# Moving a transpose stage into the arm of a branch, and hinting a jump over empty iterations

## The chip, the cores and the metric

The kernel runs on one core of a Trainium2 chip. The metric is device microseconds of one execution. A core has five engines with an instruction stream each: TensorE (PE, matmuls and transposes, with the loading of weights shown apart as PEld), VectorE (DVE), ScalarE (ACT), GpSimd (POOL) and SyncE (SP, here mostly an issuer of DMAs). A runtime branch is executed by every engine whose code it holds.

## The reference, cut to what matters

Three layers follow each other, in fp32:

```
x = attention(q, k, v)                # blocks of 64 rows
for each batch, for each position s:  # the experts, the stage of this change
    fresh = argmax(logits[s])
    e = fresh if s == 0 or gate[s] < 0.5 else e_of_the_position_before
    out[s] = softmax(logits[s])[e] * (relu(x[s] @ w1[e]) @ w2[e])
out = causal_mix(out)                 # four causal attention experts, top 2
```

There are 8 batches of 576 positions, a model width of 512, 8 experts and an inner width of 1024. Which row goes to which expert is known only at run time.

## The kernel before

The kernel first computes the attention and the routing, then the experts, then the causal mix. The change is in the experts stage, function `experts`.

The rows are sorted by expert into slots of 128 rows, and two slots make a pair. A pair belongs to one expert. The loop `pairs(2, 23)` goes over pairs t = 2 to 22; a second loop over pairs 23 to 27 stands under `tc.If(GO[NP])` (lines 1128 to 1130) for inputs that spread worse; with these inputs it is jumped over. Each pair has a kind, a number computed by the kernel itself and loaded into a register of each engine (`kind`): 0 is two full tiles of 128 rows, 1 the same with a second tile of at most 64 rows, 2 one tile, 3 ("short" below) one tile of at most 64 rows. In the run shown the short pairs are 4, 9, 11, 15 and 19; pairs 14 and 22 are of kind 1 and the others of kind 0. Products are made of two parts: every fp32 operand is split into a high and a low fp32r half (`split`, `relu_split`: one ACT and one DVE operation each), and hi x hi, lo x hi and hi x lo are summed.

The loop body is software-pipelined. In iteration t these steps are issued, in this order on every engine:

- `gather(t+2)` (POOL, indirect DMA), the gate values of t, the kind of t+1 and whether t+1 has a new expert;
- `swap(t-1, 1)`: if pair t-1 has a new expert, its W2 is split on ACT and DVE, and the next one is loaded by SP;
- `up(t)`: the product with W1, `If(KIND[t] < 2)` at line 988. The full arm has 96 matmuls per two tiles (lines 1608 to 1610 of a helper) and splits the result with a relu. The other arm has `one` (line 970), with W1 as the moving operand: 16 matmuls for a short pair, and a copy of each half of the result to `hs` (ACT, line 971). There the result lies with rows on partitions, and must be transposed;
- `x_in(t+1)`: eight transposes of the next pair's x on PE (line 939), and their split (lines 862, 863); `x_fold(t+1)` at line 951;
- `swap(t+1, 0)`: the same as above for W1 of pair t+1;
- `down(t-1)`: tile 0 of the product with W2 (lines 1016, 1018, in the arms of `either`, line 1034), its scaling and an indirect DMA to y (line 1026); then `middle`, which is `h_t` of pair t; then, under `If(KIND[t-1] < 2)` at line 1048, tile 1.

`h_t` stands under a branch of its own, line 975:

```
with tc.If(KIND[t] > 1):
    for js, p in parts:
        for j in range(4):
            nc.tensor.transpose(p[:, j, :], hs[:, ...], self.ident)   # line 978
    with tc.If(KIND[t] > 2) as half:
        ... two copies (ACT, line 981), two adds (DVE, 982), relu and split (955, 956)
```

The tile framework inserts the semaphores between engines. Each engine runs its instructions in order, so what is issued later on an engine waits behind what is issued earlier. In an arm that is not taken the semaphore increments that its instructions would have made are made up for by instructions of its own.

Behind the experts comes `causal_mix`: some masks (POOL, DVE), 30 matmuls on zeros (`keep_warm`, line 158, called at line 1216), and then a list of work in an order that a planner has set; its first loads from y (SP, line 1259) and transposes of them (PE, line 1267) follow.

Of the kernel before, what the change touches and what calls it, by code (L numbers as in the profile page):

```python
# [13 lines left out]
AF = mybir.ActivationFunctionType  # L14
OP = mybir.AluOpType
# [5 lines left out]
def as_f32(ap):  # L21
    return ap.bitcast(F32)
# [91 lines left out]
class Model:  # L114
# [785 lines left out]
    def experts(self, mix):  # L900
        nc, tc = self.nc, self.tc
# [5 lines left out]
        with ExitStack() as ctx:  # L907
# [7 lines left out]
            KIND, NEXT = {}, {}  # L915
            scat = self.scat
            rest = wk.tile([64, DM], F32, name="rest")

            def gather(t):
                XG[t] = [io.tile([128, DM], F32, name="xg", bufs=2 * AHEAD + 2) for _ in range(2)]  # L920
# [33 lines left out]
            def relu_split(hi, lo, src):  # L954
                nc.scalar.activation(hi, src, AF.Relu)  # L955
                nc.vector.scalar_tensor_tensor(lo, src, 0.0, as_f32(hi), op0=OP.max, op1=OP.subtract)  # L956

            def up(t):
                xh, xl = XH[t]
                hh, hl = HH[t] = [wk.tile([128, JF, 256], F32R, name=n, bufs=2) for n in ("hh", "hl")]  # L960
                hs = wk.tile([128, F], F32, name="hs")
                both = hs[:, :512].rearrange("p (j r) -> p j r", j=JF)
                ph = [ps.tile([128, 512], F32, name="ph", bufs=4) for _ in range(4)]
                cols = [slice(0, 4), slice(4, 8)]

                def one(terms):
                    for n, (p, fs) in enumerate(zip(ph, cols)):
                        for i, (x, w) in enumerate(terms):
                            for j in range(JD):
                                nc.tensor.matmul(p, x[:, j, :128], w[:, j, fs], start=i == j == 0, stop=i == len(terms) - 1 and j == JD - 1)  # L970
                        nc.scalar.activation(hs[:, n * 512:(n + 1) * 512], p, AF.Copy)

                def h_t():
                    parts = [(slice(4 * f, 4 * f + 4), p.rearrange("p (j r) -> p j r", j=4)) for f, p in enumerate(ph[2:])]
                    with tc.If(KIND[t] > 1):  # L975
                        for js, p in parts:
                            for j in range(4):
                                nc.tensor.transpose(p[:, j, :], hs[:, (js.start + j) * 128:(js.start + j + 1) * 128], self.ident)
                        with tc.If(KIND[t] > 2) as half:
                            for js, p in parts:  # L980
                                nc.scalar.activation(both[:, js], p[:, :, 64:], AF.Copy)
                                nc.vector.tensor_tensor(both[:, js], both[:, js], p[:, :, :64], op=OP.add)
                            relu_split(hh[:, :, :64], hh[:, :, 64:128], both)
                        with half.Else():
                            for js, p in parts:
                                relu_split(hh[:, js, :128], hl[:, js, :128], p)

                with tc.If(KIND[t] < 2) as two:
                    for c, p in enumerate(ph):
                        p = p.rearrange("p (d n) -> p d n", d=2)  # L990
                        for d in range(2):
                            self.mm3(p[:, d], [(W1[0][:, j, 2 * c + d], W1[1][:, j, 2 * c + d], xh[:, j], xl[:, j]) for j in range(JD)])
                        relu_split(hh[:, 2 * c:2 * c + 2], hl[:, 2 * c:2 * c + 2], p)
                    with tc.If(KIND[t] > 0):
                        nc.scalar.activation(hh[:, :, 192:], as_f32(hl[:, :, 128:192]), AF.Copy)
                with two.Else():
                    with tc.If(KIND[t] > 2) as half:
                        one([(xh, W1[0]), (xh, W1[1])])
                    with half.Else():
                        one([(xh, W1[0]), (xl, W1[0]), (xh, W1[1])])  # L1000
                return h_t

            def down_new(t, last):
                py = ("ph", 4) if last else ("py", 2)
                PY[t] = [[p.tile([128, DM], F32, name=n, bufs=k) for _ in range(2)] for p, (n, k) in ((ps, py), (io, ("ys", 3)))]

            def down(t, middle, ms):
                hh, hl = HH[t]
                py, ys = PY[t]
                pgs = PG[t]  # L1010

                def tile(m, half):
                    ms = slice(m * 128, (m + 1) * 128)
                    for j in range(JF):
                        for h in (hh,) if half else (hh, hl):
                            nc.tensor.matmul(py[m], h[:, j, ms], W2[0][:, j], start=h is hh and j == 0, stop=False)  # L1016
                    for j in range(JF):
                        nc.tensor.matmul(py[m], hh[:, j, ms], W2[1][:, j], start=False, stop=j == JF - 1)  # L1018
                    if half:
                        nc.scalar.activation(rest, py[m][64:], AF.Copy)  # L1020
                    nc.vector.tensor_scalar(ys[m], py[m], pgs[m], None, op0=OP.mult)  # L1021
                    if half:
                        nc.vector.scalar_tensor_tensor(ys[m][:64], rest, pgs[m][:64], ys[m][:64], op0=OP.mult, op1=OP.add)

                def put(m):
                    st = nc.gpsimd.indirect_dma_start(  # L1026
                        out=self.y_d, out_offset=bass.IndirectOffsetOnAxis(ap=self.sidx[:, 2 * t + m:2 * t + m + 1], axis=0),
                        in_=ys[m], in_offset=None, bounds_check=self.N - 1, oob_is_err=False)
                    for s in scat:
                        tc.declare_no_dep(st.ins, s.ins, reason="no two slots hold the same row")  # L1030
                    scat.append(st)

                def either(m, least):
                    with tc.If(KIND[t] < least) as full:
                        tile(m, False)
                    with full.Else():
                        tile(m, True)
                    put(m)

                if t not in KIND:  # L1040
                    for m in ms:
                        tile(m, False)
                        put(m)
                    middle()
                    return
                either(0, 3)
                middle()
                with tc.If(KIND[t] < 2):  # L1048
                    either(1, 1)

# [12 lines left out]
            def swap(t, w):  # L1063
                with tc.If(GO[t]):
                    for f in self.split_pieces((W1, W2)[w], raw[w]):
                        f()
                    load(w, t)

            def pairs(t0, t1):
# [15 lines left out]
                swap(t0, 0)  # L1085
                if first:
                    down_new(t0 - 1, False)
                    down(t0 - 1, lambda: None, [0])
                if not first:
                    swap(t0, 1)  # L1090
                for t in range(t0, t1 + 1):
                    if t + AHEAD < t1:
                        gather(t + AHEAD)
                    if t < t1:
                        gather_p(t)
                    if t + 1 < t1:
                        kind(t + 1)
                        go(t + 1)
                        x_new(t + 1)
                    if t > t0:  # L1100
                        down_new(t - 1, t == t1)

                    middle = lambda: None
                    if t < t1:
                        if extra and t >= t0 + AHEAD:
                            extra.pop(0)()
                        if t > t0 + (not first):
                            swap(t - 1, 1)
                        middle = up(t)
                    if t + 1 < t1:  # L1110
                        x_in(t + 1)
                        x_fold(t + 1)
                        swap(t + 1, 0)
                    if t > t0 or first:
                        down(t - 1, middle, [1] if t == T0 else range(2))
                    else:
                        middle()
                    if t == t1:
                        break
                    if t == T0:  # L1120
                        raw[1] = self.exp_pool.tile([128, JF, DM], F32, name="raw2")
                        load(1, 0)
                    if t == t1 - 1:
                        swap(t, 1)
                    if t == T0 + AHEAD:
                        GO[NP] = flag(self.chg[0:1, NP:NP + 1], [ET.Activation, ET.DVE, ET.Pool, ET.PE, ET.SP])

            pairs(T0, self.NF)
            with tc.If(GO[NP]):
                pairs(self.NF, NP)  # L1130

    def mix_weights(self, pool, tmp):
# [547 lines left out]
```

## Time and profile before

| | |
|---|---|
| median of three runs | 1107.15 us (1105.62 to 1107.49) |
| profiled execution | 1108.88 us |
| its span | 1107.1 us, mean granted clock 0.994 |
| PE busy | 1042.8 us, 94% |
| DVE busy | 684.6 us, 62% |
| ACT busy | 617.6 us, 56% |
| POOL busy | 337.4 us, 30% |

A share of busy time is over the whole span, and several stages with different limits lie in it. An engine that waits is shown with the instruction that released it; "PEq" or "ACTq" as a releaser is that engine's sequencer, which executes branches and semaphore instructions and counts as not busy. The experts stage of pairs 2 to 22 runs from about 240 to 694 us. The granted clock is TensorE's, as a share of full speed.

### The profile page before, as it was taken

The numbers are of one execution on the slowest core, as the hardware profiler recorded it, in microseconds if no ns is written. First come the engines' busy times: TensorE is split into PE (matmuls) and PEld (weight loads), VectorE is DVE, ScalarE is ACT, GpSimd is POOL, SyncE is SP. The second block draws the span as 40 slices with busy tenths as digits, with TensorE's granted clock in tenths as the row PEclk, the third lists the DMA queues.
The fourth block names the chain that finished last, engine by engine and source line by source line (L and its number), as shares of the span: only waits on it lengthen the run. The fifth ranks groups of instructions, "written<-read, shape, count | busy, mean of one in ns | idle before, by whom it ended". The sixth has DMA issues, their size and how long they took to land. (4 is left out here: it accounts for less than half of the span.)

```text
span 1107.1 us, 24188 instructions
## 1 busy us (share of the span) xinstructions
PE 1042.8 (94%) x7947; PEld 922.4 (83%) x7947; DVE 684.6 (62%) x1791; ACT 617.6 (56%) x1533; POOL 337.4 (30%) x586
## 2 busy tenths in 40 slices
PE   7999988999999998999999998999999999999996
PEld 5777766889888877988888887788999999999985
DVE  6678778473443244543633331387888897898884
ACT  7999997312432233423523220276777777777774
POOL 3102244233223223223332221133334333333431
PEclk9999999999999998999999999999999999999999
DMA  9988984124544134434531320345152533425231
GB/s 224 227 236 216 238 244 133 50 85 163 192 157 155 39 118 122 167 108 136 196 130 50 120 97 32 86 111 124 49 125 67 139 73 115 106 68 133 61 84 49
DMA packets 136486, 139.08 MB, mean 126 GB/s; under 512 B 54724, under 2 KB 108024, under 8 KB 134264
## 3 DMA queue, kind: packets, MB, share of 16 engines
q1 hardware_dynamic: 116584, 99.66, 33.2%
q0 software_dynamic: 12592, 35.18, 9.8%
q10 hardware_dynamic: 7136, 2.11, 0.9%
q8 instruction: 86, 1.41, 0.6%
q14 instruction: 88, 0.72, 0.2%
HBM read 89.70 MB, written 29.64 MB: 108 GB/s over the span
## 5 line engine op out<-in xcount | busy, mean ns | idle before, releaser
L1608 PE MATMUL ph<-xh,w 128*128 128x256 f32 x512 | 142.8, 279 | 6.0 <-ACTq L1048 5.2
L1610 PE MATMUL ph<-xh,w 128*128 128x256 f32 x512 | 142.5, 278 | 0.4 <-issue 0.4
L1609 PE MATMUL ph<-xl,w 128*128 128x256 f32 x512 | 142.4, 278 | 0.0
L955 ACT ACTIVATE hh<-ph 128x512 fp32r<-128x512 f32 x64 | 37.4, 598 | 183.1 <-PE ph L1610 165.3
L1026 POOL DMA_INDIRECT y_d<-ys,sidx x39 | 39.4, 1010 | 298.9 <-DVEq L975 180.4
L1016 PE MATMUL py<-w,hh 128*128 128x512 f32 x280 | 106.0, 403 | 4.7 <-PEq L975 4.7
L1441 POOL TENSOR_SCALAR a<-a,st,g_out 128x128 f32<-128x128 f32 (+3 forms) x128 | 79.0, 617 | 85.4 <-DVE st L1436 58.0
L956 DVE SCALAR_TENSOR_TENSOR hl<-ph,hh 128x512 fp32r<-128x512 f32 x64 | 43.2, 688 | 98.2 <-ACT hh L955 61.4
L1608 PEld LDWEIGHTS ph<-xh,w 128*128 128x128 f32 x512 | 96.2, 188 | 9.0 <-ACTq L1048 6.8
L1021 DVE TENSOR_SCALAR ys<-py,pg 128x512 f32<-128x512 f32 x37 | 27.7, 749 | 112.0 <-PE py L1018 64.6
L1610 PEld LDWEIGHTS ph<-xh,w 128*128 128x128 f32 x512 | 96.8, 189 | 0.1
L1609 PEld LDWEIGHTS ph<-xl,w 128*128 128x128 f32 x512 | 96.1, 188 | 0.5
L1425 ACT ACTIVATE a<-sc,st 128x256 f32<-128x256 f32 (+4 forms) x160 | 82.9, 520 | 19.7 <-DVE st L1417 14.1
L1016 PE MATMUL py<-w,hl 128*128 128x512 f32 x232 | 91.0, 392 | 0.0
L1417 DVE TENSOR_REDUCE st<-sc 128x1 f32<-128x256 f32 (+4 forms) x160 | 75.8, 482 | 4.4
L1240 ACT ACTIVATE at<-tp 128x128 fp32r<-128x128 f32 (+2 forms) x144 | 65.1, 455 | 23.2 <-PE tp L1458 21.2
L1241 DVE TENSOR_TENSOR at<-tp,at 128x128 fp32r<-128x128 f32 (+2 forms) x144 | 72.3, 505 | 7.6 <-ACT at L1240 6.4
L1458 PE MATMUL tp<-ident,a 128*128 128x128 f32 (+1 forms) x400 | 69.9, 277 | 7.0 <-DVE at L1241 3.4
L863 DVE TENSOR_TENSOR w<-raw,w 128x512 fp32r<-128x512 f32 (+1 forms) x84 | 67.1, 866 | 14.5 <-ACT w L862 11.1
L1018 PE MATMUL py<-w,hh 128*128 128x512 f32 x280 | 69.8, 392 | 0.0
L1016 PEld LDWEIGHTS py<-w,hh 128*128 128x128 f32 x280 | 52.4, 189 | 19.0 <-issue 8.9
L1406 PE MATMUL sc<-kd,qs 128*128 128x128 f32 (+3 forms) x256 | 62.7, 337 | 4.9 <-ACT a L1425 3.4
(338 smaller groups left out, 2922.3 us busy)
## 6 DMA issues: line engine op xcount, KB each, us to landing
raw<-in_moe_w_dram SPq DMA_DIRECT2D x32, 1024.0 KB
kd<-kb SPq DMA_DIRECT2D x64, 160.0 KB
vb<-in_v_dram SPq DMA_DIRECT2D x144, 64.0 KB
x_d<-xs POOLq DMA_DIRECT2D x36, 256.0 KB
yt<-y_d SPq DMA_DIRECT2D x32, 256.0 KB
kd<-kb SPq DMA_DIRECT2D x64, 128.0 KB
out_dram<-zs SPq DMA_DIRECT2D x32, 256.0 KB
q<-in_q_dram SPq DMA_DIRECT2D x11, 512.0 KB
```

The costliest lines, as they stand in the source:

```text
L863: (engine or self.nc.vector).tensor_tensor(lo, src, as_f32(hi), op=OP.subtract)
L1016: nc.tensor.matmul(py[m], h[:, j, ms], W2[0][:, j], start=h is hh and j == 0, stop=False)
L1018: nc.tensor.matmul(py[m], hh[:, j, ms], W2[1][:, j], start=False, stop=j == JF - 1)
L1240: h = plan.add("ACT", act(n), lambda: A.activation(hi, src(), AF.Copy), key, dep)
L1241: l = plan.add("DVE", dve(n), lambda: V.tensor_tensor(lo, src(), as_f32(hi), op=OP.subtract), key, [h])
L1417: V.tensor_reduce(st[:, i:i + 1], box["sc"][i][:, :k1 - k0], axis=AX.X, op=OP.max, negate=True)
L1425: A.activation(a[:, k0:k1], box["sc"][i][:, :k1 - k0], AF.Exp, bias=st[:, 0:1], accum_out=st[:, 3 + i:4 + i])
L1441: (P if ext <= PX else V).tensor_scalar(a[:, :ext], a[:, :ext], st[:, 6:7], gate, op0=OP.mult, op1=OP.mult)
L1458: nc.tensor.transpose(ta[:c1 - c0, kc - k0], box["a"][:, c0:c1], self.ident)
L1608: self.nc.tensor.matmul(out, ah, bh, start=first and i == 0, stop=False)
L1609: self.nc.tensor.matmul(out, ah, bl, start=False, stop=False)
L1610: self.nc.tensor.matmul(out, al, bh, start=False, stop=last and i == n - 1)
```

## The change

The transposes of the next pair's x move from behind `up(t)` into both arms of its branch: `up` gets them as a function `then`, called at the end of each arm. `h_t` moves from the middle of `down(t-1)` to the end of the arm for one tile, directly behind them, and loses its own `If`; `down` loses its `middle`. So in a short pair, h_t's transposes, copies, adds and relu are issued before the W1 swap and before the down projection's first tile; in a full pair nothing is left of it. The list of all five engines gets a name, and the branch over pairs 23 to 27 gets a label and a hint: ahead of the last down projection of the first loop a hint instruction on each of the five engines names that branch and the register that decides it. The causal stage is unchanged.

```diff
-            def up(t):
+            def up(t, then):
...
 
                 def h_t():
                     parts = [(slice(4 * f, 4 * f + 4), p.rearrange("p (j r) -> p j r", j=4)) for f, p in enumerate(ph[2:])]
-                    with tc.If(KIND[t] > 1):
+                    for js, p in parts:
+                        for j in range(4):
+                            nc.tensor.transpose(p[:, j, :], hs[:, (js.start + j) * 128:(js.start + j + 1) * 128], self.ident)
+                    with tc.If(KIND[t] > 2) as half:
                         for js, p in parts:
-                            for j in range(4):
-                                nc.tensor.transpose(p[:, j, :], hs[:, (js.start + j) * 128:(js.start + j + 1) * 128], self.ident)
-                        with tc.If(KIND[t] > 2) as half:
-                            for js, p in parts:
-                                nc.scalar.activation(both[:, js], p[:, :, 64:], AF.Copy)
-                                nc.vector.tensor_tensor(both[:, js], both[:, js], p[:, :, :64], op=OP.add)
-                            relu_split(hh[:, :, :64], hh[:, :, 64:128], both)
-                        with half.Else():
-                            for js, p in parts:
-                                relu_split(hh[:, js, :128], hl[:, js, :128], p)
+                            nc.scalar.activation(both[:, js], p[:, :, 64:], AF.Copy)
+                            nc.vector.tensor_tensor(both[:, js], both[:, js], p[:, :, :64], op=OP.add)
+                        relu_split(hh[:, :, :64], hh[:, :, 64:128], both)
+                    with half.Else():
+                        for js, p in parts:
+                            relu_split(hh[:, js, :128], hl[:, js, :128], p)
...
                 with tc.If(KIND[t] < 2) as two:
                     for c, p in enumerate(ph):
@@ -993,18 +993,20 @@
                         relu_split(hh[:, 2 * c:2 * c + 2], hl[:, 2 * c:2 * c + 2], p)
                     with tc.If(KIND[t] > 0):
                         nc.scalar.activation(hh[:, :, 192:], as_f32(hl[:, :, 128:192]), AF.Copy)
+                    then()
                 with two.Else():
                     with tc.If(KIND[t] > 2) as half:
                         one([(xh, W1[0]), (xh, W1[1])])
                     with half.Else():
                         one([(xh, W1[0]), (xl, W1[0]), (xh, W1[1])])
-                return h_t
+                    then()
+                    h_t()
...
-            def down(t, middle, ms):
+            def down(t, ms):
...
-                    middle()
                     return
                 either(0, 3)
-                middle()
                 with tc.If(KIND[t] < 2):
                     either(1, 1)
...
-                    middle = lambda: None
                     if t < t1:
                         if extra and t >= t0 + AHEAD:
                             extra.pop(0)()
                         if t > t0 + (not first):
                             swap(t - 1, 1)
-                        middle = up(t)
+                        up(t, lambda: t + 1 < t1 and x_in(t + 1))
                     if t + 1 < t1:
-                        x_in(t + 1)
                         x_fold(t + 1)
                         swap(t + 1, 0)
+                    if t == t1 and first:
+                        tc.mark_branch_hint_location("more", hint=GO[NP], engines=TAIL)
                     if t > t0 or first:
-                        down(t - 1, middle, [1] if t == T0 else range(2))
-                    else:
-                        middle()
...
             pairs(T0, self.NF)
-            with tc.If(GO[NP]):
+            with tc.If(GO[NP], label="more"):
                 pairs(self.NF, NP)
```

## Rows read from the trace of the kernel before

**Rows 1.** Page, part 1: busy us of each engine (share), instructions.

```profile
PE 1042.8 (94%) x7947; PEld 922.4 (83%) x7947; DVE 684.6 (62%) x1791; ACT 617.6 (56%) x1533; POOL 337.4 (30%) x586
```

**Rows 2.** Waits of PE, 262 to 704 us: total, times, longest.

```profile
PE ph L1608 <- ACTq L1048: 5.2, 4, 1.5
PE tp L158 <- DVEq L1129: 4.8, 1, 4.8
PE py L1016 <- PEq L975: 4.7, 10, 0.6
PE ph L970 <- ACT w L862: 3.7, 1, 3.7
```

**Rows 3.** Line 975, PE's sequencer: count, ns min/median/max, first and last start.

```profile
L975 PEldq EVENT_SEMAPHORE  x16: 51/51/51, 269.0 to 673.6; - x16
```

**Rows 4.** Timeline of PE, pairs 3 and 4: start, us, line, [idle <-releaser].

```profile
288.77 0.49 PE L1016 MATMUL py<-w,hh 128*128 128x512 f32 x1 [0.44 <-PEq L975]
...
304.51 1.04 PE L978 MATMUL ph<-ident,hs 128*128 128x128 f32 x8
305.30 0.48 PE L1016 MATMUL py<-w,hh 128*128 128x512 f32 x1
```

**Rows 5.** Timeline of PE, start of pair 6.

```profile
327.93 0.36 PE L1608 MATMUL ph<-xh,w 128*128 128x256 f32 x1 [1.26 <-ACTq L1048]
```

**Rows 6.** Timeline of PE, start of pair 11, and pair 15.

```profile
430.46 2.00 PE L1018 MATMUL py<-w,hh 128*128 128x512 f32 x8
436.12 6.34 PE L970 MATMUL ph<-w,xh 128*128 128x512 f32 x16 [3.65 <-ACT w L862]
442.30 1.11 PE L939 MATMUL pxt<-ident,xg 128*128 128x128 f32 x8
...
520.02 3.83 PE L970 MATMUL ph<-w,xh 128*128 128x512 f32 x16
```

**Rows 7.** Stretch: length, busy us of PE, PEld, DVE, ACT, POOL, clock, DMA, GB/s.

```profile
436.12:442.30 6.18, 6.18 (x17) 4.81 (x17) 4.99 (x8) 3.99 (x8) 4.01 (x4) 0.56 0.82 250
```

**Rows 8.** Line 988, PE's branch, columns as in rows 3.

```profile
L988 PEldq COMPARE_BRANCH  x21: 65/71/2867, 247.4 to 652.9; - x21
```

**Rows 9.** Timeline of ACT, 434 to 443 us.

```profile
435.24 4.27 ACT L862 ACTIVATE w<-raw 128x512 fp32r<-128x512 f32 x8 [2.08 <-DVEq L1048]
439.87 0.60 ACT L971 ACTIVATE hs<-ph 128x512 f32<-128x512 f32 x1 [0.36 <-ACT w L862]
```

**Rows 10.** Timelines of ACT, DVE and PE, pair 15 and start of 16.

```profile
526.02 3.90 ACT L862 ACTIVATE w<-raw 128x1024 fp32r<-128x1024 f32 x4 [0.50 <-DVE xl L863]
530.84 0.77 ACT L981 ACTIVATE hs<-ph 128x256 f32<-128x256 f32 x2 [0.91 <-PE ph L978]
533.10 0.63 ACT L955 ACTIVATE hh<-hs 128x512 fp32r<-128x512 f32 x1 [1.49 <-DVE hs L982]
...
527.12 4.63 DVE L863 TENSOR_TENSOR w<-raw,w 128x1024 fp32r<-128x1024 f32 x4 [0.82 <-ACT w L862]
...
532.33 0.74 DVE L982 TENSOR_TENSOR hs<-hs,ph 128x256 f32<-128x256 f32 x2
...
534.71 0.28 PE L1608 MATMUL ph<-xh,w 128*128 128x256 f32 x1
```

**Rows 11.** Line 1129, sequencers of PE and DVE, columns as in rows 3.

```profile
L1129 PEldq COMPARE_BRANCH  x1: 3456/3456/3456, 684.9 to 684.9; - x1
...
L1129 DVEq EVENT_SEMAPHORE  x2: 21/21/21, 693.7 to 693.8; - x2
```

**Rows 12.** Timelines of DVE and PE, end of the expert stage.

```profile
690.42 0.74 DVE L1023 SCALAR_TENSOR_TENSOR ys<-rest,pg,ys 64x512 f32<-64x512 f32 x1
...
693.76 8.34 PE L158 MATMUL tp<-zeros 128*128 128x512 bf16 x30 [4.85 <-DVEq L1129]
```

**Rows 13.** Stretches before the causal stage, columns as in rows 7.

```profile
699.00:699.60 0.60, 0.60 (x5) 0.24 (x4) 0.00 (x0) 0.00 (x0) 0.19 (x2) 1.00 0.35 133
699.60:700.20 0.60, 0.60 (x4) 0.26 (x3) 0.00 (x0) 0.00 (x0) 0.00 (x0) 1.00 0.05 17
```

More of the change, by code (lines that the diff above doesn't have):

```diff
@@ L917, in experts @@
             rest = wk.tile([64, DM], F32, name="rest")
+            TAIL = [ET.Activation, ET.DVE, ET.Pool, ET.PE, ET.SP]
             def gather(t):
@@ L1087, in pairs @@
                     down_new(t0 - 1, False)
-                    down(t0 - 1, lambda: None, [0])
+                    down(t0 - 1, [0])
                 if not first:
@@ L1108, in pairs @@
                             swap(t - 1, 1)
-                        middle = up(t)
+                        up(t, lambda: t + 1 < t1 and x_in(t + 1))
                     if t + 1 < t1:
-                        x_in(t + 1)
                         x_fold(t + 1)
                         swap(t + 1, 0)
+                    if t == t1 and first:
+                        tc.mark_branch_hint_location("more", hint=GO[NP], engines=TAIL)
                     if t > t0 or first:
-                        down(t - 1, middle, [1] if t == T0 else range(2))
-                    else:
-                        middle()
+                        down(t - 1, [1] if t == T0 else range(2))
                     if t == t1:
@@ L1125, in pairs @@
                     if t == T0 + AHEAD:
-                        GO[NP] = flag(self.chg[0:1, NP:NP + 1], [ET.Activation, ET.DVE, ET.Pool, ET.PE, ET.SP])
+                        GO[NP] = flag(self.chg[0:1, NP:NP + 1], TAIL)
             pairs(T0, self.NF)
-            with tc.If(GO[NP]):
+            with tc.If(GO[NP], label="more"):
                 pairs(self.NF, NP)
```

## The prediction

> **What bounds the kernel now.** I read the busy shares of the page first: TensorE (PE) is busy 94% of the span and the next engine, VectorE (DVE), 62% [rows 1]. So a microsecond counts only if PE stands idle or slow in it, and the page is not fine enough for that. The list of PE's waits over the expert stage (262 to 704 us) gives what there is to win: 4.7 us in ten waits at line 975, 5.2 us in four waits at line 1048, one wait of 3.7 us before line 970, and one of 4.8 us at the end of the stage, with little beside them [rows 2]. The reader is to see that nearly all of PE's idle time in the stage ends at a branch or at an arm that is jumped over, and little of it at data. The change touches each of these four places.
>
> **Part 1, the skipped arm of line 975 goes away.** Pairs 2 to 22 run here. Five are short (4, 9, 11, 15, 19); in the other sixteen the arm of line 975 is skipped, and the skip is not free: each engine then runs a semaphore instruction in the arm's place, on PE sixteen times [rows 3]. It is put down to PE's own queue: PE waits there until its own earlier matmuls have ended. The ordinary case is the first row of [rows 4]: tile 1 of the down projection starts 0.44 us after the last matmul of tile 0, where matmuls otherwise overlap. Where the arm is taken (pair 4) there is no such gap: the eight transposes of line 978 start at 304.51, last 1.04, and tile 1 starts at 305.30, before they have ended [rows 4]. So the cost is the drain at the skip, 0.47 us on average (4.7 over ten). After the change both arms hold real work (the full arm ends in the transposes of the next x, the short one in h_t's), so no arm without instructions is left at this place. That gives -4.7 us. PE's work as such is the same: the x transposes are issued once in whichever arm runs, h_t's eight likewise. Bounds: 0 if the drain shows up at another join, -4.7 if not; a loss is excluded, as no instruction is added on the path. I take -4.7, since the taken arm's row shows a join without a gap.
>
> In the six skips not among the ten, the next PE work is not tile 1 of the same pair. One (in pair 2) is covered by a wait for weights. In the five others the pair before was short, so the skip of line 975 is followed by that of line 1048: PE drains twice, loads the next pair's kind and branches before it gets work. Four of these end in the waits of line 1048, 5.2 us in all; the first is [rows 5], 1.26 us. The change takes away one of the two drains and leaves the other. The second drain finds PE empty anyway, so what goes is one semaphore instruction and one branch in series. The nearest row prices that at 0.47 as in the ten; the bounds are 0 and the whole 1.26. I take 0.47 x 4 = -1.9 us.
>
> **Part 2, the fifth of these, before pair 11.** Here pair 9's half tile has drained PE and pair 11 is short, so PE must also jump over the whole full arm. Its last matmul ends at 430.46 + 2.00 = 432.46, and the 16 matmuls of line 970 start at 436.12, 3.65 us later; they then take 6.34 us where the same 16 of pair 15 take 3.83 [rows 6]. [...] The wait is put down to a ScalarE copy of line 862 that was long done, so it is something that this row doesn't name. A jump that takes long is the best candidate: the PE branch of line 988 has a median of 71 ns but once took 2867 [rows 8]. The change removes the drain of line 975 ahead (-0.5 us), but the jump over the full arm remains and becomes longer, by the eight transposes now in that arm. I keep the stall: -0.5 us. If it vanishes, PE starts some 2.8 us earlier at full clock, but then h_t can't run at once: it needs the copies of line 971, and ScalarE splits the new W2 from 435.24 for 4.27 us before it makes the first of them at 439.87 [rows 9]. PE would have reached h_t near 438 and would wait until about 440.5 for it. Of the 2.8 + 2.5 us about 2.5 stay. So this place lies between -3 and 0.
>
> [...]
>
> **Part 3, h_t and the W1 swap.** In a short pair h_t now comes before the W1 swap (all five short pairs are followed by a new expert). ScalarE's and VectorE's part of it: two copies of 0.77 us together, two adds of 0.74, the relu of 0.63 [rows 10], a chain of 2.1 us now ahead of the swap instead of behind it. Does PE wait for it? The tightest is pair 15: the swap runs on ScalarE from 526.02 and on VectorE from 527.12 for 4.63, until 531.75; pair 16 starts at 534.71 [rows 10]. Shifted by 2.1 it ends at 533.85, with 0.9 us to spare. So this costs nothing; if the cover were gone, it would be as many tenths as the swap is later than 2.1 + 0.9 us. PE itself must wait for the second copy of line 971 (0.6 us) before the second half of h_t; the eight x transposes (1.1 us) lie between. Cost 0, bounds 0 to +0.5 a pair. On SyncE (SP) and GpSimd (POOL) there is nothing in the moved code but the branch; POOL's scatters are issued behind one branch fewer.
>
> **Part 4, the hint for the jump over pairs 23 to 27.** VectorE's last work ends at 690.42 + 0.74 = 691.16, and its first semaphore instruction behind the jump runs at 693.7; PE stands until 693.76 for that and nothing else, 4.85 us in all [rows 11, 12]. PE's own branch (3456 ns at 684.9) lies beside matmuls that it had already queued. If the hint makes VectorE's target ready, PE's warming matmuls (30, 8.34 us) start at about 691.3, or 2.4 us earlier. What is late next is the first block of y for the causal stage: its loads wait for the last scatter, which the hint doesn't move, and their traffic runs at 133 GB/s until 699.60 and at 17 after it [rows 13]. The warming ends at 702.1 now and would end at 699.7, so both fit: -2.3 us. Bounds: 0 (no effect) to -2.9 (the block that is needed first has landed by 699.0, and the warming is over by then). The row with VectorE's 2.5 us between branch and next instruction is the nearest one, so I take -2.3. [...]
>
> **Sum.** -4.7 - 1.9 - 0.5 - 2.3 = -9.4 us. Against the profiled execution (1108.88, of which 1107.1 is the span) that is 1099.5; the median of the three runs lies 1.7 lower, at 1107.15, and from it I get 1097.7. The causal stage behind is as before and only starts earlier.
>
> **Rivals.**
> [...]
> 2. The stall before pair 11 goes as well. For it: every instruction behind the first pair moves in memory, and such a stall was seen at one of five places only. Against: the jump is longer. Time: 2.5 lower, 1095.2.
> 3. The drains of line 975 come back in another place, as the full arm and the short arm end in different instructions and one of them is evened out by a semaphore instruction behind the x transposes. For it: such instructions stand in every skipped arm. Against: behind the short arm the x transposes follow without a gap today (442.30, before the last of line 970 has ended [rows 6]), though the arms are unequal. [...]
> 4. Slower: the late W1 swap stalls PE at the start of all five pairs behind short ones. For it: relu and adds of h_t cross between ScalarE and VectorE, and the swap stands behind the last of them. The price of one place is the wait and, if PE drops to the low clock as in [rows 7], the 2.5 us that 6.34 against 3.83 shows. It decides from 9.4 / 5 = 1.9 us a place, that is from a swap 2.1 + 0.9 + 1.9 = 4.9 us later than now without a drop of the clock; with 2 us of wait and the drop it is 5 x 4.5 - 9.4 = 13 us slower, 1120. Against: the chain of rows is 2.1 us, and pair 15 alone has as little room as 0.9.
>
> **How the numbers follow.** Forecast 0.52, rival 1 0.18, rival 2 0.12, rival 3 0.10, rival 4 0.05, remainder (mixtures, small losses) 0.03. The range runs from 1094.5 (rival 2 with the larger gain of the hint) to 1103 (rival 1 with a wait of 1 us at three of the pairs of part 3), and leaves out most of rivals 3 and 4. A measurement of this kernel can tell about 0.2%, 2.2 us, from no change: faster (under 1104.9) is the forecast, rivals 1 and 2 and half of rival 3, 0.88; same 0.06; slower 0.06.
>
> **What would show it.** Right: PE's waits for its own queue at line 975 are gone and nothing of 0.4 us stands ten times in their place; the four waits of line 1048 are near 0.8 us each; the warming matmuls start within 0.3 us of VectorE's last work; PE starts pairs 5, 10, 12, 16 and 20 without waiting for a weight copy. Wrong: a drain behind the x transposes (rival 3), VectorE still 2.5 us late behind the last jump (rival 1), waits for line 863 ahead of line 1608 in those five pairs (rival 4), a new long stall before a short pair's line 970. A time over 1104.9 makes the prediction wrong as a whole.

## The result, and the profile after

The changed kernel takes 1090.57 us (1088.82 to 1091.69, five runs) where the kernel before takes 1105.62 in the same series: 0.9859 of it, interval [0.9844, 0.9873], 15 us less. The forecast was 1097.7, the lower end of the range 1094.5. The direction and the places were right and the size was not; 5.6 us were missing, on a forecast of 9.4.

The profiled execution took 1090.41 us. First the engines (busy us, share, instructions), to be read beside [rows 1]:

```profile
PE 1039.2 (95%) x7947; PEld 922.9 (85%) x7947; DVE 684.7 (63%) x1791; ACT 617.1 (57%) x1533; POOL 336.8 (31%) x586
```

PE has the same 7947 matmuls, and yet 3.6 us less busy time: the first hint that more went than the idle time shows. The waits of PE from 262 to 704 us (total, times, longest), beside [rows 2]:

```profile
PE ph L1606 <- ACTq L1048: 3.4, 4, 0.9
PE tp L158 <- DVEq L1127: 2.6, 1, 2.6
PE ph L971 <- ACTq L1048: 1.5, 1, 1.5
PE ph L978 <- ACT hs L972: 1.2, 1, 1.2
```

The reader is to see four things. The ten waits for PE's own queue are gone and nothing has come in their place. The four places behind a short pair have fallen from 5.2 to 3.4 us. The wait before pair 11 is 1.5 and not 3.7 us. And there is one new wait, of 1.2 us, for `hs` (line 978 is h_t's transposes). The matmul lines have moved by two: 1606 to 1608 are the former 1608 to 1610, 1018 and 1020 the former 1016 and 1018.

What the skipped arm had cost is seen best where tile 0 meets tile 1. The timeline of PE in pair 6, first before, then after (start us, length, [idle before it <- released by]):

```profile
344.71 0.85 PE L1018 MATMUL py<-w,hh 128*128 128x512 f32 x3
346.02 0.49 PE L1016 MATMUL py<-w,hh 128*128 128x512 f32 x1 [0.45 <-PEq L975]
346.35 0.40 PE L1016 MATMUL py<-w,hl 128*128 128x512 f32 x1
```

```profile
339.84 1.08 PE L1020 MATMUL py<-w,hh 128*128 128x512 f32 x4
340.76 0.39 PE L1018 MATMUL py<-w,hh 128*128 128x512 f32 x1
340.99 0.39 PE L1018 MATMUL py<-w,hl 128*128 128x512 f32 x1
```

After the change a matmul starts every 0.23 us though one lasts 0.39, as they overlap. Before, the last of the three of line 1018 started at about 345.17 (346.02 - 0.45 - 0.40), and from there to the first of tile 1 it was 0.85 us, and 0.33 to the next. Against 0.23 and 0.23 that is 0.62 + 0.10 = 0.72 us, where the idle column says 0.45. The rest is booked as busy time: the tail of the last matmul and the slow first one overlap with nothing.

Pair 11 after the change, beside [rows 6], and ScalarE there, beside [rows 9]:

```profile
425.70 3.92 PE L971 MATMUL ph<-w,xh 128*128 128x512 f32 x16 [1.45 <-ACTq L1048]
429.46 1.11 PE L940 MATMUL pxt<-ident,xg 128*128 128x128 f32 x8
431.77 1.15 PE L978 MATMUL ph<-ident,hs 128*128 128x128 f32 x8 [1.21 <-ACT hs L972]
433.17 0.47 PE L1018 MATMUL py<-w,hh 128*128 128x512 f32 x1 [0.24 <-issue]
```

```profile
426.82 4.28 ACT L862 ACTIVATE w<-raw 128x512 fp32r<-128x512 f32 x8 [1.88 <-PE ph L971]
431.12 1.08 ACT L972 ACTIVATE hs<-ph 128x512 f32<-128x512 f32 x2
```

There is no stall of 3.7 us and no low clock: the 16 matmuls take 3.92 us, and from 425.70 to 429.46 the granted clock is 1.00. h_t waits for the copies that stand behind the split of W2, as part 2 had it for a stall that goes, but 1.2 us and not 2.5.

The W1 swap of pair 15 on VectorE and the first PE work of pair 16, beside [rows 10]:

```profile
516.42 4.63 DVE L863 TENSOR_TENSOR w<-raw,w 128x1024 fp32r<-128x1024 f32 x4 [1.00 <-ACT w L862]
```

It ends at 521.05 and pair 16 starts at 521.70 without a wait; 0.65 us to spare, 0.9 were forecast. The last jump, beside [rows 11, 12], VectorE's first semaphore instruction behind it and PE's warming matmuls:

```profile
L1127 PEldq COMPARE_BRANCH  x1: 351/351/351, 668.1 to 668.1; - x1
...
L1127 DVEq EVENT_SEMAPHORE  x2: 21/21/21, 674.6 to 674.8; - x2
```

```profile
673.67 0.74 DVE L1025 SCALAR_TENSOR_TENSOR ys<-rest,pg,ys 64x512 f32<-64x512 f32 x1
```

```profile
674.73 8.34 PE L158 MATMUL tp<-zeros 128*128 128x512 bf16 x30 [2.56 <-DVEq L1127]
```

VectorE's last work ends at 674.41 and PE starts 0.3 us later; before it was 2.6 us. With the hint VectorE's first semaphore instruction behind the jump runs at 674.6, 0.2 us after its last work, instead of 2.5, and PE's own branch takes 351 ns instead of 3456, hidden both times behind matmuls that run to 672.16 and 688.92.

### The profile page after: what moved, and what is told of

Same layout as the page of the kernel before. It is cut to its first block, busy times and chain, and to the rows that moved or that the text cites. A ratio compares the mean times of both kernels' runs of the same rounds, so it can differ in the third digit from the quotient of the medians.

```text
span 1088.6 us, 23980 instructions
## 1 busy us (share of the span) xinstructions
PE 1039.2 (95%) x7947; PEld 922.9 (85%) x7947; DVE 684.7 (63%) x1791; ACT 617.1 (57%) x1533; POOL 336.8 (31%) x586
## 5 line engine op out<-in xcount | busy, mean ns | idle before, releaser
L863 DVE TENSOR_TENSOR w<-raw,w 128x512 fp32r<-128x512 f32 (+1 forms) x84 | 67.1, 866 | 15.7 <-ACT w L862 11.2
L862 ACT ACTIVATE w<-raw 128x512 fp32r<-128x512 f32 (+1 forms) x84 | 57.3, 762 | 16.7 <-DMA wst<-in_moe_wq_dram 6.0
```

The lines of the kernel that those rows point to most:

```text
L863: (engine or self.nc.vector).tensor_tensor(lo, src, as_f32(hi), op=OP.subtract)
```

## Experiments

Each ran against the kernel before, in four series, each on a chip of its own by the record: e1 to e4 in series 1, e5 to e8 in series 2, r1, e9, e10 and e12 in series 3, e13, e14 and r2 in series 4. In series 1 and 3 the kernel before takes 1105.9 and 1105.7 us, in series 2 and 4 1111.3 and 1111.8. Times are compared within a series; across series only the ratios to the kernel before are, and with care.

**The hint alone, the move alone** (series 1).

```diff
+ tc.mark_branch_hint_location("more", hint=GO[NP], engines=TAIL)   # e1: added to the kernel before
- tc.mark_branch_hint_location("more", hint=GO[NP], engines=TAIL)   # e2: taken from the changed kernel
```

> The kernel before with the label and the hint alone; x_in, h_t and the branch of line 975 as they were. Theory (the drains at skipped arms are most of the gain, the hint is the small part): VectorE's 2.5 us behind the last jump go, PE's idle time ahead of the warming matmuls falls from 4.8 to about 2.5 us, the ten waits at line 975 stay at 4.7 us and the stall before pair 11 at 3.7; the time is 2.3 to 2.7 us lower, about 1103. Rival A (the hint brings the 5.6 us that the forecast lacked): about 1097. Rival B (the hint does nothing): 1105.6.

> The changed kernel without the hint and the label. Theory: all drains of line 975 gone, the stall before pair 11 gone as in the changed kernel (the hint stands behind that place in the program), VectorE 2.5 us late behind the last jump as before: 2.3 to 2.7 us above the changed kernel, about 1093. Rival A (the hint brings the excess): about 1099. Rival B (the hint does nothing): 1090.6.

e1 takes 1103.24 us, 0.998 [0.9969, 0.9991]; its ten waits at the skipped arm are there (4.9 us), and PE's wait before the warming is 2.5. e2 takes 1093.26, 0.989 [0.9876, 0.9904]. So the hint is worth about 2.6 us and the move 12.6, and they add up to the 15. The move was forecast at 7.1, so the excess over the forecast is in it.

**One half of the move at a time** (series 1). e3 puts x_in into both arms and leaves h_t in the middle under its branch; e4 moves h_t and leaves x_in behind the join.

```diff
-                        middle = up(t)
+                        middle = up(t, lambda: t + 1 < t1 and x_in(t + 1))   # e3; h_t and its If as before
...
-                    then()
-                    h_t()
+                    h_t()          # e4; x_in(t + 1) again behind up(t)
```

> The kernel before with x_in in both arms of the branch of up, and nothing else: h_t stays in the middle of the down projection under its branch at line 975, no hint. Theory (drains): the ten waits at the skipped arm stay at 4.7 us, so no gain from them; only the stall before pair 11 may go, as code moves: 1105.6 or, without the stall, 1101 to 1103. Rival (the transposes of x in the arms are themselves a gain, by a join fewer on the path of the transposes): at least 5 us lower, 1100 or less, with the waits at line 975 in place.

> The changed kernel with x_in back behind the join of the branch of up, so h_t stands in the short arm directly behind the product, no hint. Theory: no skipped arm is left in the middle, so the ten drains are gone (7 us by the distance from matmul to matmul, 0.72 a place), but in the five short pairs PE has no x transposes to do while ScalarE copies the second half of the product (0.6 us and the way there), so it stands about 0.8 us in each, 4 us in all: 1105.6 - 7 - 1.5 + 4 = about 1101, or 1098.5 if the stall before pair 11 goes. Rival (the gain comes with the x transposes in the arms): near 1105.

e3: 1101.37 us, 0.9964 [0.9951, 0.9977]. Waits of PE and the start of pair 11:

```profile
PE py L1018 <- PEq L975: 4.5, 10, 0.5
PE ph L970 <- DVE ys L1023: 1.8, 1, 1.8
```

```profile
430.46 3.92 PE L970 MATMUL ph<-w,xh 128*128 128x512 f32 x16 [1.84 <-DVE ys L1023]
```

The drains are all there, and 4.2 of the 4.5 us come from pair 11 (34.18 us from the start of pair 10 to that of pair 12, 38.41 before): the stall is 1.8 instead of 3.7 us, and the 16 matmuls take 3.92 instead of 6.34. The full stall was gone although the jump over the full arm had become longer. e4: 1098.41 us, 0.9931 [0.9918, 0.9944], near the theory without the stall (1098.5). No drain is left, but five waits for `hs` come up, 3.0 us in all, 0.25 in four pairs and 2.0 in pair 11. The x transposes between product and h_t are PE's cover for ScalarE's copy: e4 differs from e2 in their place alone and is 5.2 us slower.

**The same program, its code elsewhere** (series 2). 64 matmuls on PE in an arm that is never taken, ahead of the loop.

```diff
                     down_new(t0 - 1, False)
+                    with tc.If(KIND[t0] > 1):
+                        self.keep_warm(PY[t0 - 1][0][0], 64)
```

> The kernel before with 64 matmuls on PE in an arm that is never taken, ahead of the loop over pairs: nothing that runs in the loop changes, but its PE code lies 128 or more instructions further on. Theory (the stall before pair 11 hangs on where the code lies): the wait of 3.7 us there falls under 2, the slow clock behind it goes, pairs 10 and 11 together take some 4 us less; the drains stay at 4.7 us; about 1102 with some 0.7 for the skipped arm. Rival (the stall comes from what waits there: the drain of line 975 and ScalarE's order): 3.7 us as before, 1106.

1109.31 us against 1111.29, 0.9981 [0.9969, 0.9993]. Pair 11:

```profile
437.37 5.50 PE L970 MATMUL ph<-w,xh 128*128 128x512 f32 x16 [1.85 <-DVE ys L1021]
```

The stall is halved with nothing else changed ahead of it, so half of it hangs on where the code lies. The expected 4 us didn't come, only 2: the slow stretch is still there in part (5.50 us), and pair 5 now has small issue waits of its own.

**A skipped arm put back, for PE alone** (series 2).

```diff
                 either(0, 3)
+                with tc.If(KIND[T0] > 1):
+                    self.keep_warm(py[1], 1)
                 with tc.If(KIND[t] < 2):
```

> The changed kernel with a branch on PE in the middle of the down projection whose arm (one matmul on zeros) is never taken, in all 21 pairs: only PE gets a skip back, ScalarE and VectorE do not. Theory (a skip costs PE the distance 0.84 to 0.95 instead of 0.23 us from matmul to matmul and a slow second one, 0.72 together): 15 places with a tile 1 behind them by 0.72 and five behind a short pair by 0.36, +12.6 us, about 1103. Rival A (the skip costs what the idle column shows, 0.47 and 0.4): +9, 1099.6. Rival B (most of the gain came from ScalarE and VectorE being free of the skip): +3 or less.

1109.71 us, 0.999 [0.9976, 1.0003]. The changed kernel didn't run in this series; e7 below, which differs from it in the hint's engines alone, takes 1099.11. So some 11 us are lost to a branch that only PE pays for. Its waits:

```profile
PE py L1018 <- PEq L1048: 7.3, 15, 0.7
```

The idle column shows 7.3 us in 15 places, 0.49 each, while the iterations of full pairs are 0.7 to 0.9 us longer than those of the changed kernel (23.75 to 22.89 between the starts of pairs 7 and 8). Rival B is out. The time lies between rival A (9 us) and the theory (12.6) and can't tell them apart; the lengths of the iterations, 0.7 to 0.9 longer where the idle column shows 0.49, speak for the theory.

**The hint on VectorE alone** (series 2).

```diff
- hint=GO[NP], engines=TAIL
+ hint=GO[NP], engines=[ET.DVE]
```

> The changed kernel with the hint on VectorE alone. Theory (PE's start behind the last jump waits for VectorE only, and VectorE's instructions were what was late): as the changed kernel, 1090.6, PE's idle time ahead of the warming matmuls 2.6 us. Rival (the hint on PE or ScalarE matters): 1092 to 1093.3, as without a hint.

1099.11 us, 0.9901 [0.9888, 0.9914]; the changed kernel in series 4, on a chip with a like time of the kernel before, 0.9893 [0.9872, 0.9914]. The sequencers at the last jump:

```profile
L1127 DVEq EVENT_SEMAPHORE  x2: 21/21/21, 681.2 to 681.4; - x2
L1127 ACTq EVENT_SEMAPHORE  x2: 17/17/17, 681.6 to 681.7; - x2
...
L1127 PEldq COMPARE_BRANCH  x1: 3669/3669/3669, 674.7 to 674.7; - x1
L1127 ACTq COMPARE_BRANCH  x1: 50/50/50, 679.0 to 679.0; - x1
L1127 DVEq COMPARE_BRANCH  x1: 85/85/85, 680.6 to 680.6; - x1
```

PE's branch is long again and ScalarE is 2.6 us late again, but VectorE is not, and PE's wait before the warming is 2.6 us as with all five. By the waits VectorE is the one that counts; the times of two series alone would not show it.

**No empty arm behind a short pair, three ways.** e8 (series 2) puts both tiles of the down projection into one branch, e10 (series 3) is e8 with its code moved as in e5, e9 (series 3) gives PE one matmul on zeros in an else arm of line 1048. r1 is the changed kernel beside them, e12 the changed kernel with its code moved (both series 3).

```diff
-                with tc.If(KIND[t] < 2):             # e8, e10
+                with tc.If(KIND[t] < 2) as two:
+                    tile(0, False)
+                    put(0)
                     either(1, 1)
+                with two.Else():
+                    either(0, 3)
...
                 with tc.If(KIND[t] < 2) as two:      # e9
                     either(1, 1)
+                with two.Else():
+                    self.keep_warm(py[1], 1)
```

> The changed kernel with the down projection's two tiles in one branch: tile 0 and tile 1 in the arm for two tiles, the half or single tile in the other, so that the branch of line 1048 has no skipped arm left behind a short pair. Theory: the waits of 3.4 us in four and 1.5 us in one place go, and with them the distance lost from matmul to matmul (about 1.1 us a place and 1.5 for pair 11): 5 to 6 us lower, 1085. Rival A (PE must load the kind and branch there anyway, and stands for it): 1 to 2 us lower, 1089. [...]

> The kernel with both tiles of the down projection in one branch, its PE code 128 instructions further on (64 matmuls in an arm that is never taken, ahead of the loop). [...] Rival (the long arms themselves stall): the wait of 3.4 us behind pair 15 stays, and the time is within 2 us of the changed kernel or above it.

> The changed kernel with one matmul on zeros in an else arm of line 1048, so that PE, and PE alone, skips no empty arm behind a short pair. Theory (an arm with an instruction needs no semaphore instruction that waits for PE's own queue): the waits of 3.4 us in four places and 1.5 in one fall to what ScalarE's skip leaves (it runs some 0.7 us behind PE's last matmul), 2 to 5 us lower than the changed kernel. Rival A (PE stands there for ScalarE's copy of the half tile and not for its own queue): within 1 us of the changed kernel, same waits. Rival B (the matmul's arm costs more than the skip): 1 to 2 us higher.

> The changed kernel with its PE code 128 instructions further on in the same way (about 0.7 us for the skipped arm). Theory (what the forecast lacked at pair 11 hangs on where the code lies, the drains don't): no waits at skipped arms in the middle of the down projection, as in the changed kernel; the start of pair 11 and other starts may stall by 1 to 4 us each; 1 to 6 us above the changed kernel, or the same if no stall comes up. Rival (pair 11's stall went for good with the drain of line 975): 0.7 us above, no stall over 1.5 us at pair 11.

> The changed kernel once more, beside the variants of it. [...] Rival (a good part of the first result is luck of one build on one chip): 10 us or less.

e8: 1102.01 us, 0.9912 [0.9895, 0.9929], 2.9 us above e7 beside it. The waits of line 1048 are gone, but others are new, the longest of them these:

```profile
PE py L1018 <- issue: 3.7, 2, 3.4
...
PE ph L978 <- ACT hs L972: 2.2, 1, 2.2
```

The wait of 3.4 us lies in the down projection of pair 15. In e10 it is gone, and one of 2.9 before pair 15's product has come up instead: 1093.55 us, 0.9896 [0.9877, 0.9914], above r1 with 1089.69, 0.9855 [0.984, 0.9871]. r1 is 16.0 us under the kernel before beside it, so its rival is out. So such a stall moves with the code: e8 is slower than e7, where its theory and rival A had it faster, and in e10 the stall doesn't stay behind pair 15 as the rival had it, though e10's time is no better. e9: 1089.22 us, 0.9852 [0.9835, 0.9869], not to be told from r1. Its waits of line 1048 are gone, and in pair 11 h_t waits for `hs` 2.7 us instead of 1.2, as PE is there sooner and ScalarE is not; the transposes then take 1.97 us instead of 1.15.

The gain behind the short pairs is partly lost again: pair 6 starts 15.60 us behind pair 5 (16.57 in r1), but pair 7 23.47 behind pair 6 (22.97), and from pair 10 to pair 12 it is 36.75 (35.73). The transposes of pair 11:

```profile
431.65 1.97 PE L978 MATMUL ph<-ident,hs 128*128 128x128 f32 x8 [2.66 <-ACT hs L972]
```

e12: 1090.67 us, 0.9861 [0.9838, 0.9883]: the gain of the change doesn't hang on one placing of its code; pair 11 has no stall over 1.5 us in it, as the rival said.

**The drain taken away, h_t left where it was** (series 4). e13 is the kernel before with an else arm at line 975; e14 is the same with e9's else arm and the hint; r2 is the changed kernel.

```diff
-                    with tc.If(KIND[t] > 1):
+                    with tc.If(KIND[t] > 1) as many:
...
+                    with many.Else():
+                        self.keep_warm(ph[0], 1)
```

> The kernel before with an else arm at line 975 that holds one matmul on zeros for PE, and nothing else: h_t stays where it was, ScalarE and VectorE still skip, no hint. Theory (the cost is PE's drain in an arm without an instruction, not the place of h_t): the ten waits for PE's own queue at line 975 go; 0.72 us less and 0.23 more for the matmul in each, so 5 us lower, 1100.5, plus or minus what the stall before pair 11 does. Rival (the arm's semaphores for ScalarE and VectorE hold PE up, or h_t's place is what counts): waits at tile 1 stay, time within 1.5 us of the kernel before.

> The same, with one matmul on zeros in an else arm of line 1048 too, and the hint: the kernel before with all its empty PE arms filled, h_t left in the middle of the down projection. Theory: 5 us from line 975, 4 times about 1.1 and 1.5 from line 1048, 2.6 from the hint, and in pair 11 h_t does not wait for ScalarE's split of W2 as it does in the changed kernel: 13 to 15 us lower than before, 1091, within 2 us of the changed kernel; below it if the stall before pair 11 goes. Rival (moving h_t into the arm is worth something by itself): 3 us or more above the changed kernel.

> The changed kernel beside these two: 1089 to 1091 where the kernel before takes 1105.7.

e13: 1101.07 us, 0.9891 [0.987, 0.9912], 10.7 us less with one matmul more in each pair that isn't short. The waits of line 975 are gone; pair 11 starts after 1.4 us, and its 16 matmuls take 3.92 us. By the profiles (that of before is from another series) the ten places make some 5 us of it (23.19 us from pair 6 to pair 7, 23.70 before), and pair 11, whose stall also moves with the code, 4.4 (33.99 from pair 10 to pair 12, 38.41 before):

```profile
PE ph L1610 <- ACTq L1050: 3.3, 4, 0.8
PE ph L970 <- DVE ys L1023: 1.4, 1, 1.4
```

e14: 1091.8 us, 0.9819 [0.9804, 0.9834], the lowest ratio of all; r2 beside it 1099.16, 0.9893 [0.9872, 0.9914]. The pair 11 of e14:

```profile
432.46 2.19 PE L971 MATMUL ph<-w,xh 128*128 128x512 f32 x8
434.84 2.09 PE L971 MATMUL ph<-w,xh 128*128 128x512 f32 x8 [0.18 <-DVEq L976]
```

PE goes from the half tile into pair 11 without a stop, and h_t, still behind tile 0, finds its copies made. Rival out: with h_t left in the middle the kernel isn't 3 us above the changed one but 7.4 below it. Not all of that is h_t's place, as the changed kernel lacks the else arm of line 1048; with it, it is e9, which ran in another series (0.9852). In pair 11 the moved h_t costs its wait: from pair 10 to pair 12 it is 32.97 us in e14, 36.75 in e9 and 36.17 in r2. r2 missed its expectation, which was written for series with a faster kernel before; in series 4 the change brings 12.7 us. Why less than the 15 to 16 of the other series stays open.

## Why the prediction was right and where it was wrong

**Part 1, the skipped arm: right in mechanism, mis-sized.** The step that failed is "So the cost is the drain at the skip, 0.47 us on average (4.7 over ten)", and with it the bound of 4.7. The idle column gave the size, and it counts from the end of a matmul that would have overlapped with the next. From start to start a drain costs 0.72 us, and the ten together 7.5 (the two tiles take 11.49 to 11.70 us from the first start to the last before, 10.76 to 10.85 after), so 2.8 us were missing. The changed kernel's loop shows it: pair 6 to pair 7 took 23.70 us (327.93 to 351.63) and takes 22.95 (323.31 to 346.26). e6 and e13 show it from both sides. The semaphore instruction in the arm's place runs sixteen times each on PE (51 ns), ScalarE (17) and VectorE (21), not on every engine.

**The skip in pair 2: put at nothing, wrong.** "One (in pair 2) is covered by a wait for weights" failed. From the start of pair 2 to that of pair 3 it took 18.78 us (251.06 to 269.84) and takes 17.77 (248.39 to 266.17). Here is the start of pair 3 on PE and VectorE's split of its W1, first before, then after:

```profile
267.02 1.98 PE L1018 MATMUL py<-w,raw 128*128 128x512 f32 x8
269.84 0.36 PE L1608 MATMUL ph<-xh,w 128*128 128x256 f32 x1 [0.84 <-DVE w L863]
...
266.03 4.63 DVE L863 TENSOR_TENSOR w<-raw,w 128x1024 fp32r<-128x1024 f32 x4 [0.67 <-ACT w L862]
```

```profile
264.35 1.98 PE L1020 MATMUL py<-w,raw 128*128 128x512 f32 x8
266.17 0.28 PE L1606 MATMUL ph<-xh,w 128*128 128x256 f32 x1
...
263.21 4.63 DVE L863 TENSOR_TENSOR w<-raw,w 128x1024 fp32r<-128x1024 f32 x4 [0.68 <-ACT w L862]
```

After the change pair 3 starts 2.96 us behind the start of the split, and without a wait. By that the weights would have let it start at 268.99 before, when PE's matmuls ended (269.00); PE's semaphore instruction of line 975 runs there, at 269.0 [rows 3], and pair 3 starts 0.84 us later. So the wait was put down to the wrong engine, and this skip cost 1.0 us. The four kernels with the empty arm of line 975 show 18.78 to 18.87 us here (before, e1, e3, e5), all others 17.77 to 17.82.

**The four places behind short pairs: right.** Forecast 1.9, measured 1.8 by the waits (5.2 to 3.4). The second drain does remain.

**Part 2, pair 11: wrong.** "I keep the stall: -0.5 us" failed; rival 2 came about. From the start of pair 10 to that of pair 12 it took 38.41 us and takes 35.72, so 2.7 and not 0.5. Under it lies a misread row, "A jump that takes long is the best candidate". The long branch of [rows 8] stands ahead of pair 9, beside queued matmuls (pair 9 waits 0.22 us), and not ahead of pair 11:

```profile
L988 PEldq COMPARE_BRANCH  x1: 2867/2867/2867, 396.9 to 396.9; - x1
...
L988 PEldq COMPARE_BRANCH  x1: 208/208/208, 433.7 to 433.7; - x1
```

So the jump ahead of pair 11 was over in 0.2 us, and PE loaded the first weights of line 970 at 434.28. Its first matmul started at 436.12 [rows 6], 1.84 us behind that load; in e5 it is 0.04 us (before, then e5):

```profile
434.28 0.19 PEld L970 LDWEIGHTS ph<-w,xh 128*128 128x128 f32 x1 [2.25 <-issue]
...
437.33 0.19 PEld L970 LDWEIGHTS ph<-w,xh 128*128 128x128 f32 x1 [2.25 <-issue]
437.37 0.95 PE L970 MATMUL ph<-w,xh 128*128 128x512 f32 x3 [1.85 <-DVE ys L1021]
```

The DMA view of before has a packet in a queue of the kind "instruction" here (433 to 436.1 us: packets, MB, share):

```profile
q8 instruction: 1, 0.02, 2.2%
```

What it held, and whether PE stood for it, no run shows. What the runs show is that the long part of the stall hangs on where the code lies (e5, 3.7 to 1.85 with the same loop; e8 against e10). Nor is it the length of the jump: e3's is longer and doesn't stall in full. The first weights were loaded 0.4 us after the jump here, so the stall came behind it. The copy of line 862 that the wait is put down to isn't what PE needed: in the changed kernel PE starts at 425.70, ahead of the first such copy (426.82). What the forecast gave for the drain itself fits: about 1.85 us of wait with both drains (e3, e5), 1.2 to 1.5 with one (the changed kernel, e12, e13), 0.2 with none (e14). The slow stretch doesn't follow from the length of the wait alone: behind 3.65 us the 16 matmuls take 6.34, at a granted clock of 0.56 [rows 7], behind e3's 1.84 they take 3.92, and behind e5's 1.85 they take 5.50.

**Part 3: right.** Order and swap cost nothing (0.65 us to spare), and the x transposes cover the second copy of `hs` in four of the five short pairs, as e4 shows by its lack of them; in pair 11, where W2's split stands ahead of the copy, they don't (1.2 us).

**Part 4: right.** 2.3 us were forecast, 2.6 measured by e1, 2.3 by the wait (4.85 to 2.56), with VectorE as the engine that decides (e7).

The terms as measured, 7.5 + 1.0 + 1.8 + 2.7 + 2.6, make 15.6, where the medians differ by 15.05 and the interval of the ratio leaves 14 to 17. The two profiles differ by more, 18.5 us of span; 2.7 of that lie ahead of pair 2, where the change alters nothing. Rivals 1 (a hint without effect, 1100.0), 3 (the drains in another place, 1104.9) and 4 did not come about. The chances named for a faster time add up to 0.87, not 0.88.

## What to carry to other kernels

Price an idle gap in a stream of overlapped matmuls from start to start (here 0.72 us), not by the idle column (0.45), and look at whether busy time falls too. A runtime branch with an arm that held nothing for PE drained PE here, and one matmul in that arm removed the drain without moving any work (e13); that is worth trying before a restructuring. Before you put a gap at nothing because the profile names another engine, look at when that engine was done, and look up where in time a row with a maximum stands. After any edit of code under runtime branches, look for stalls that belong to the placing of the code, and judge an idea by more than one placing.

## What the runs showed of the hardware that was not expected

One matmul of 0.39 us in an otherwise empty arm saves PE about 0.5 us net (e13). From its first matmul to the next stage a full product takes 10.90 to 10.99 us in most pairs and 11.2 to 11.4 in others, without a wait in it, at a granted clock of 1.00 and with the same code; which pairs are slow differs from profile to profile (7, 8, 14 and 20 before, 12, 17 and 21 after). Two stretches of the kernel before (length, busy PE, PEld, DVE, ACT, POOL, clock, DMA):

```profile
351.63:362.93 11.30, 11.30 (x97) 11.30 (x96) 2.73 (x4) 1.68 (x3) 4.83 (x5) 1.00 0.22 73
327.93:338.92 10.99, 10.99 (x97) 10.99 (x97) 8.85 (x14) 6.92 (x12) 5.63 (x5) 1.00 0.41 127
```

Both run the same arm, 96 matmuls, and the slower one has less going on beside it. Its cause stays open; with three or four such pairs it is some 1.5 us in a run, no more than the runs of one kernel scatter (1105.52 to 1107.49). It isn't part of the terms above.
